# Values of the first pair asked for on two queues, and the loads of keys, queries and weights paced in single pieces

## Chip, cores and metric

One core of a Trainium2 chip runs the whole program. The metric is the device time of one launch in microseconds (us); three runs of the kernel before gave a median of 244.76 us (243.74 to 244.88).

## What is computed

The inputs are 32-bit floats. First comes attention in chunks: each chunk of 32 tokens sees 16 tokens to its left, itself, 8 to its right and 8 memory keys. Then each of the 3072 tokens goes through a dense pair of matrices and through the one expert of eight that a gate picks for it.

```python
for c in range(nc):
    k_ctx = k[:, :, max(0, 32*c - 16):min(S, 32*c + 40)]     # v_ctx alike
    k_full = np.concatenate([mem_k, k_ctx], axis=2)           # v_full alike
    a = softmax(scale * q_c @ k_full.T)
    out[:, :, 32*c:32*c + 32] = a @ v_full
x = out as [3072 tokens, 512]
y = relu(x @ w1_dense) @ w2_dense
e = argmax(x @ w_gate);  p = softmax(x @ w_gate)[e]
y += p * (relu(x @ w1[e]) @ w2[e])
```

Four batches, 8 heads of 64 numbers, 768 tokens in a batch; 8 experts of 512 x 512 and 512 x 512.

## The kernel before

The program has two stages. The **attention stage** is a loop over 24 tiles `i` of 128 tokens (6 to a batch), written as a software pipeline: in round `i` TensorE (PE) makes the scores of tile `i`, turns the exponent's input of tile `i-1` (`turn`), multiplies tile `i-2` with its values (`values`, L612), and turns the finished tile `i-3` for the gate (`turn_x`). Each engine takes its instructions in the order written, and TensorE therefore stops at the first product whose input is late. VectorE (DVE) does the row maxima, subtraction and normalisation (L592, L594, L621, L623), ScalarE (ACT) the exponential (L603) and copies out of PSUM, GpSimd (POOL) the copies in the value tiles and a cast (L629).

**Values.** Two tiles make a pair with one buffer `vw` (four buffers in turn: in the program's lists `vw_133` is the first pair's, `vw_134` the second's, and so on). A pair's values come in eight pieces, four heads in each of two halves (`load_v`, L489; a batch's first pair has four small ones more, L487 and L488), asked for on SyncE's (SP's) queue. Before them `put_mem` (L468) fills the buffer with memory rows on ACT, for the second pair on POOL. The right context of a chunk is the next chunk's rows: `shift_v` copies them inside the buffer, a long copy for either half of the partitions (L505) and, for the pair's last chunk, a short one from the next pair's buffer (L508). The product of the pair's first tile needs its two long copies. That of the second tile needs the two short ones, and so the next pair's values.

**Keys and queries** of a batch (`load_part`, L431) are asked for on POOL, turned to bf16 on the way, and land in `wall`, where later the weights of three experts lie. A batch has 16 pieces of 192 KB, in half-heads: two of keys, two of queries, and the same for the other heads. TensorE turns them a batch ahead (`transposes`, L537), in eight steps per batch, `LATE` for the second batch (two steps in each of rounds 2 to 5), `EVEN` for the others. The first batch's are turned ahead of the loop, with idle products `spin` in between.

**Order.** `pieces` is a list of loads; `piece()` is called four times in a round and issues the next one, or nothing where the entry is `None`. In rounds 0 to 10 `ask_qk` adds two pieces of keys or queries (`QK_AT`), in rounds 12, 13, 15, 17, 19 and 21 `ask_w` adds two pieces of weights (`W_AT`). POOL thus has loads, copies and casts in one line of work.

The **expert stage** takes slots of 128 tokens; each has a dense and an expert half. The products of a slot's second matrices go to two PSUM banks, ACT copies the one to `o`, VectorE adds the other one times the gate's weight (L265), and POOL scatters `o` to the output (L266). The last slot that runs is `tail`.

Of the kernel before, what the change touches and what calls it, by code (L numbers as in the profile page):

```python
# [14 lines left out]
ALU = mybir.AluOpType  # L15
# [40 lines left out]
W_ORDER = [E] + list(range(E))  # L56
W_AT = (12, 13, 15, 17, 19, 21)
QK_AT = tuple(range(11))


@with_exitstack
def kernel(
# [175 lines left out]
    def y_of(j, half):  # L238

        if j == tail and half:  # L240
            return xp[:, 0] if place_of(j) else sc[0]
        return sc[half] if place_of(j) else xp[:, half]
# [16 lines left out]
    def s_exp2(j, w):  # L259
        s_second(j, w, "he", 1)  # L260

    def s_send(j):
        o = w3.tile([128, DM], F32, tag="o", name="o")
        nc.scalar.copy(o, y_of(j, 0))
        nc.vector.scalar_tensor_tensor(o, y_of(j, 1), gws.pop(j), o, op0=ALU.mult, op1=ALU.add)  # L265
        i = nc.gpsimd.indirect_dma_start(  # L266
            out[:, :], bass.IndirectOffsetOnAxis(ap=where.pop(j), axis=0),
            o, None, bounds_check=NTOK - 1, oob_is_err=False)
        for x in sent:
            tc.declare_no_dep(i.ins, x.ins, reason="different rows of out")  # L270
        sent.append(i)
# [131 lines left out]
    with ExitStack() as one:  # L403
# [31 lines left out]

        pieces = []

        def ask_qk():
            if qk_todo:
                a = qk_todo.pop(0)  # L440
                pieces.extend([lambda: load_part(*a, 0, 2), None, lambda: load_part(*a, 2, 2)])

        def ask_w():
            a = w_todo.pop(0)
            pieces.extend([lambda: load_w(*a, 0, 2), None, lambda: load_w(*a, 2, 2)])

# [28 lines left out]

        def load_v(n, half, after=None):
            if n >= B * NP:
# [4 lines left out]
            for hp in range(2 * half, 2 * half + 2):  # L482
                for par in range(2):
                    r = 64 * par
                    if p == 0 and hp == 0:
                        hs_ = v[b].rearrange("(a c) s d -> c s a d", c=2)[par]
                        nc.sync.dma_start(vw[r + LEFT:r + 32, 0, :, :D], hs_[0:LEFT])  # L487
                        nc.sync.dma_start(ves[b][r:r + LEFT, :, :D], hs_[S - LEFT:S])  # L488
                    dma = nc.sync.dma_start(  # L489
                        vw[r:r + 32, lo:, hp, :D],  # L490
# [289 lines left out]
        pool_constants()  # L780
        put_mem(1, nc.gpsimd.tensor_copy)
        load_part(*qk_todo.pop(0), 0, 4)

# [9 lines left out]
        for n, step in enumerate(steps):  # L793
# [6 lines left out]
            if n == 0:  # L800
                put_mem(0, nc.scalar.copy)
            if n == 3:
                load_v(0, 0, i)
                load_v(0, 1)
                load_v(1, 0)
                load_v(1, 1)
                for b in range(1, B):
                    load_mem_rows(b)
# [10 lines left out]
        for i in range(NT):  # L819
# [18 lines left out]
            mine = steps[two[t][0]:two[t][1]] if steps else []  # L838
            if i in QK_AT:
                ask_qk()  # L840
            if i in W_AT:
                ask_w()
            piece()
            if i % 2 == 0:
                if i:
                    load_v(i // 2 + 1, 1, tiles[i - 3]["pace"] if i > 3 else None)
            else:
                load_v(i // 2 + 2, 0)
# [13 lines left out]
            do("turn", 1)  # L862
            if mine:
                mine[0]()
            if ga:
                gate(ga)
            do("turn_x", 3)
            if mine[1:]:
                mine[1]()
# [25 lines left out]
            if gd and gd["n"] < EG - 1:  # L895
                add_up(gd)
            for step in mine[2:]:
                step()
            if 1 <= i <= E:
                last_constants(i - 1)  # L900
            piece()
            if i < NT - 2:
                shift_v(i // 2, i % 2, False, nc.scalar.copy if i == 1 else nc.gpsimd.tensor_copy)
            if i % 2 == 0:
                put_mem(i // 2 + 2, nc.scalar.copy)
            if i == 1:
                for e in range(E):
                    nc.gpsimd.tensor_copy(wgp[:, :, e:e + 1], wgr[:, :, PERM[e]:PERM[e] + 1])
            if NT - 3 <= i < NT - 1:
# [117 lines left out]
```

## Time and profile before

| what | value |
|---|---|
| runs, median (range) | 244.76 us (243.74 to 244.88) |
| the profiled execution's own time | 243.71 us |
| its span, first to last instruction | 242.0 us |
| PE, DVE, ACT, POOL busy | 87%, 60%, 57%, 68% |
| mean granted TensorE clock | 0.959 |
| DMA | 35.46 MB in packets, 147 GB/s |
| values in the chain that ended last (DMA `vw`) | 9% of the span |

A busy share is a mean over both stages; each stretch has its own limit. The attention stage fills about the first 130 us, the expert stage the rest. Where a row names an engine after an arrow, that is what the waiting instruction waited for last. Queue q0 carries what POOL asks for, q1 what SP asks for.

### The profile page before, as it was taken

To read this page: it belongs to the slowest core of one execution; us is meant where nothing else is said; L and a number is where in the kernel's file an instruction comes from. 1 tells how busy PE (TensorE), PEld (TensorE's weight loads), DVE (VectorE), ACT (ScalarE), POOL (GpSimd) and SP (SyncE) were. 2 spreads that over 40 slices of the span, in tenths; PEclk is the share of its full clock that TensorE was granted. 3 is DMA by queue.
4 is the path that set the end of the run, shared out by engine and by line. 5 is a ranking of instruction groups with operands and counts; after the bars stand their busy time and mean duration, and the time that the engine had idled before them with its cause. 6 is when DMAs were issued, how large, how long until landed. Compare 5 with 4: busy or idle time off the path is not lost.

```text
span 242.0 us, 9891 instructions
## 1 busy us (share of the span) xinstructions
PE 210.0 (87%) x4093; PEld 152.5 (63%) x4093; DVE 144.8 (60%) x413; ACT 137.0 (57%) x201; POOL 165.7 (68%) x228
## 2 busy tenths in 40 slices
PE   8874899887977978867889988989999999999990
PEld 3443676665755756655667766667777777777750
DVE  7656577476555856938967577366533425666650
ACT  6863977977849759516543355433444544444440
POOL 7943999969938956979596048787777653764332
PEclk9999799999979799979799999999999999999997
DMA  5997999997994983896539715999999980322112
GB/s 71 181 166 149 154 195 169 190 164 114 200 163 87 219 134 75 132 234 111 123 91 187 167 60 122 171 205 209 258 186 218 230 226 17 144 81 77 55 43 82
DMA packets 52515, 35.46 MB, mean 147 GB/s; under 512 B 29676, under 2 KB 50158, under 8 KB 52464
## 3 DMA queue, kind: packets, MB, share of 16 engines
q0 software_dynamic: 22080, 25.22, 57.8%
q1 hardware_dynamic: 30384, 9.54, 17.6%
q8 instruction: 34, 0.56, 1.0%
q14 instruction: 17, 0.14, 0.2%
HBM read 41.45 MB, written 10.24 MB: 214 GB/s over the span
## 4 chain that ended last, share of the span: by engine, by line
PE 46%; DMA 16%; DVE 11%; POOL 9%; issue 8%; SPq 4%; ACT 3%; POOLq 0%; DVEq 0%; ACTq 0%
DMA vw<-in_v_dram 9%; PE xp L247 8%; PE xtp L232 7%; PE ap L232 7%; PE sc L247 6%; PE xp L612 5%; POOL vw L505 4%; DMA out_dram<-o,idx 3%; SPq L489 3%; PE xtp L633 2%; PE ap L601 2%; DMA wall<-in_q_dram 2%; DMA xg<-xs,ixt 2%; PE tp L218 2%; DVE xn L623 2%
## 5 line engine op out<-in xcount | busy, mean ns | idle before, releaser
L232 PEld LDWEIGHTS <-wall 128*128 128x128 bf16 x672 | 40.4, 98 | 6.4 <-issue 0.4
L505 POOL COPY vw<-vw 24x1820 f32<-24x1820 f32 x21 | 35.6, 1696 | 8.6 <-DMA vw<-in_v_dram 7.5
L612 PE MATMUL xp<-vw,aT 64*32 64x65 f32 x1536 | 27.5, 234 | 12.5 <-POOL vw L508 5.2
L612 PEld LDWEIGHTS xp<-vw,aT 64*32 64x32 f32 x1536 | 20.1, 110 | 19.7 <-POOL vw L508 7.2
L235 ACT ACTIVATE hd<-ap 128x512 bf16<-128x512 f32 x26 | 15.5, 597 | 28.8 <-PE ap L232 27.6
L220 DVE COPY xT<-tp 128x512 bf16<-128x512 bf16 x24 | 10.2, 423 | 32.7 <-PE tp L218 31.5
L232 PE MATMUL ap<-xT,wall 128*128 128x128 bf16 x416 | 27.5, 219 | 0.0
L235 ACT ACTIVATE he<-xtp 128x512 bf16<-128x512 f32 x26 | 15.6, 598 | 14.8 <-PE xtp L232 14.7
L266 POOL DMA_INDIRECT out_dram<-o,ixt x12 | 13.6, 1137 | 15.0 <-DVE o L265 10.9
L603 ACT ACTIVATE aT<-ap 128x512 f32<-128x512 f32 x24 | 14.4, 599 | 15.3 <-PE ap L601 15.3
L621 DVE RECIPROCAL rs<-xp 128x8 f32<-128x8 f32 x24 | 5.0, 206 | 28.6 <-PE xp L612 28.6
L468 ACT COPY vw<-memt 128x2080 f32<-128x2080 f32 x11 | 21.3, 1935 | 0.1
L537 PEld LDWEIGHTS <-wall 128*64 128x64 bf16 x384 | 12.6, 116 | 10.4 <-issue 5.7
L202 POOL DMA_INDIRECT xg<-xs,ixt x12 | 12.8, 1066 | 8.9 <-PE ap L232 5.8
L546 ACT COPY kt<-tp 64x768 bf16<-64x768 bf16 x22 | 17.4, 791 | 2.0 <-PE tp L537 1.7
L601 PE MATMUL ap<-identf,a 128*128 128x128 f32 x96 | 17.7, 313 | 0.9 <-DVE low L178 0.5
L633 PE MATMUL xtp<-identf,xn 128*128 128x128 f32 x96 | 17.3, 309 | 0.9 <-DVE xn L623 0.5
L623 DVE TENSOR_TENSOR xn<-xp,rs 128x512 f32<-128x512 f32 x24 | 16.6, 692 | 2.3
L113 POOL DMA_DIRECT2D wall<-in_moe_w_dram x23 | 17.7, 778 | 0.0
L629 POOL CAST rows<-xn 128x512 bf16<-128x512 f32 x24 | 14.7, 619 | 3.8 <-DVE xn L623 1.9
L594 DVE TENSOR_TENSOR a<-sc,mx 128x512 f32<-128x512 f32 x24 | 16.6, 691 | 0.8
L592 DVE TENSOR_REDUCE mx<-sc 128x8 f32<-128x512 f32 x24 | 16.4, 683 | 0.3
(163 smaller groups left out, 470.8 us busy)
## 6 DMA issues: line engine op xcount, KB each, us to landing
wall<-in_moe_w_dram POOLq DMA_DIRECT2D x9, 512.0 KB, 8.8
vw<-in_v_dram SPq DMA_DIRECT2D x64, 64.0 KB, 4.3
wall<-in_moe_w_dram POOLq DMA_DIRECT2D x14, 256.0 KB, 6.3
xs<-rows SPq DMA_DIRECT2D x6, 514.0 KB, 4.8
wall<-in_q_dram POOLq DMA_DIRECT2D x16, 192.0 KB, 5.9
wall<-in_k_dram POOLq DMA_DIRECT2D x14, 192.0 KB, 4.9
vw<-in_v_dram SPq DMA_DIRECT2D x32, 56.0 KB, 5.1
wall<-in_moe_w_dense_dram POOLq DMA_DIRECT2D x4, 256.0 KB
```

The costliest lines, as they stand in the source:

```text
L113: nc.gpsimd.dma_start(wall[:, e, DT * half + t0:DT * half + t0 + nt], src.rearrange("(t p) m -> p t m", p=128)[:, t0:t0 + nt])
L232: nc.tensor.matmul(ph[:, f, :], w[:, d, 128 * f:128 * f + 128], xT[:, d, :], start=(d == 0), stop=(d == DT - 1))
L235: nc.scalar.activation(h, ph, AF.Relu)
L247: nc.tensor.matmul(y_of(j, half), h[:, f, :], w[:, f, :], start=(f == 0), stop=(f == FT - 1))
L468: copy(vws[n].rearrange("p c h d -> p c (h d)"), memt[:, n // NP].rearrange("p h d -> p (h d)").unsqueeze(1) .to_broadcast([128, PC, HP * ...
L505: eng(vw[r + 32:r + 56, :PC - 1], vw[r:r + 24, 1:])
L546: done.append(eng(kt[r, hp, par, LEFT:LEFT + S].rearrange("d (p i) -> d p i", i=TPB), turned[r]))
L594: nc.vector.tensor_tensor(a.rearrange("p h q m -> p (h q) m"), scv, mx.unsqueeze(2).to_broadcast([128, H, KEYS]), ALU.subtract)
L601: nc.tensor.transpose(ap[:, hp, :], st["a"][:, hp], identf)
L612: nc.tensor.matmul(xp[32 * cc:32 * cc + 32, par, (D + 1) * hp:(D + 1) * (hp + 1)], st["aT"][r, hp, 32 * cc:32 * cc + 32], vw[r, 4 * (g % 2 ...
L623: st["pace"] = nc.vector.tensor_tensor(xn.rearrange("p (h a d) -> p a h d", a=2, d=D), xv[:, :, :, :D], rs.unsqueeze(3).to_broadcast([128, ...
L633: nc.tensor.transpose(xtp[:, d, :], st["xn"][:, 128 * d:128 * d + 128], identf)
```

## The change

The second half of the first pair's values is asked for on POOL's queue, ahead of its fill of the second pair's buffer and of the second batch's keys and queries; the first half stays on SP. POOL's fill and those loads come behind it in the code. ACT copies the first pair's second half of the partitions in round 0 instead of 1, ahead of the first exponential, and fills the third pair's buffer in round 1 instead of 0; that pair's first half is asked for after this fill. In round 2 the two turning steps come behind the values product. Eight small POOL copies (`wgp`) become five on VectorE. Keys, queries and weights are asked for by numbers: `QK_PIECES` gives the pieces of keys and queries added in rounds 0 to 14 (2, 0, 3, 3, 1, 1, 2, ...), and from round 10 on a round with fewer than two adds one piece of weights until there are twelve. The second product of the last slot goes to two banks by halves of 256 columns, and VectorE adds each by itself.

```diff
--- before.py
+++ after.py
@@ -54,8 +54,8 @@
 NVB = 4
 NXG = 6
 W_ORDER = [E] + list(range(E))
-W_AT = (12, 13, 15, 17, 19, 21)
-QK_AT = tuple(range(11))
+QK_PIECES = (2, 0, 3, 3, 1, 1, 2, 1, 1, 2, 1, 1, 2, 1, 1)
+W_FROM, W_PIECES = 10, 12
 
 
 @with_exitstack
@@ -236,9 +236,6 @@
         hs[j, nm] = h
 
     def y_of(j, half):
-
-        if j == tail and half:
-            return xp[:, 0] if place_of(j) else sc[0]
         return sc[half] if place_of(j) else xp[:, half]
 
     def s_second(j, w, nm, half):
@@ -257,12 +254,24 @@
         s_second(j, wall[:, E, DT:], "hd", 0)
 
     def s_exp2(j, w):
-        s_second(j, w, "he", 1)
+        if j != tail:
+            return s_second(j, w, "he", 1)
+        h = hs.pop((j, "he"))
+        for x, y in enumerate(y_parts(j)):
+            for f in range(FT):
+                nc.tensor.matmul(y, h[:, f, :], w[:, f, 256 * x:256 * x + 256],
+                                 start=(f == 0), stop=(f == FT - 1))
+
+    def y_parts(j):
+        return (xp[:, 0] if place_of(j) else sc[0])[:, :256], ap.rearrange("p a n -> p (a n)")[:, :256]
 
     def s_send(j):
         o = w3.tile([128, DM], F32, tag="o", name="o")
         nc.scalar.copy(o, y_of(j, 0))
-        nc.vector.scalar_tensor_tensor(o, y_of(j, 1), gws.pop(j), o, op0=ALU.mult, op1=ALU.add)
+        gw = gws.pop(j)
+        for x, y in enumerate(y_parts(j) if j == tail else [y_of(j, 1)]):
+            part = o[:, 256 * x:256 * x + 256] if j == tail else o
+            nc.vector.scalar_tensor_tensor(part, y, gw, part, op0=ALU.mult, op1=ALU.add)
         i = nc.gpsimd.indirect_dma_start(
             out[:, :], bass.IndirectOffsetOnAxis(ap=where.pop(j), axis=0),
             o, None, bounds_check=NTOK - 1, oob_is_err=False)
@@ -433,16 +442,29 @@
                 src[b, 4 * h + n0:4 * h + n0 + n].rearrange("h (p i) d -> p h (i d)", p=128))
 
 
-        pieces = []
-
-        def ask_qk():
-            if qk_todo:
-                a = qk_todo.pop(0)
-                pieces.extend([lambda: load_part(*a, 0, 2), None, lambda: load_part(*a, 2, 2)])
-
-        def ask_w():
-            a = w_todo.pop(0)
-            pieces.extend([lambda: load_w(*a, 0, 2), None, lambda: load_w(*a, 2, 2)])
+        pieces, qk_parts, w_parts = [], [], []
+
+        def plan(i):
+            n = QK_PIECES[i] if i < len(QK_PIECES) else 0
+            mine = []
+            for _ in range(n):
+                if not qk_parts and qk_todo:
+                    a = qk_todo.pop(0)
+                    qk_parts.extend(lambda a=a, x=x: load_part(*a, x, 2) for x in (0, 2))
+                if qk_parts:
+                    mine.append(qk_parts.pop(0))
+            if i >= W_FROM and n < 2 and w_count[0] < W_PIECES:
+                if not w_parts:
+                    a = w_todo.pop(0)
+                    w_parts.extend(lambda a=a, x=x: load_w(*a, x, 2) for x in (0, 2))
+                mine.append(w_parts.pop(0))
+                w_count[0] += 1
+            for p in mine:
+                pieces.extend([p, None])
+            if pieces and pieces[-1] is None:
+                pieces.pop()
+
+        w_count = [0]
 
         def piece():
             if pieces:
@@ -473,7 +495,7 @@
             tc.add_manual_dep(dma.ins, ins.ins.name, mybir.DependencyInfo(
                 mybir.DependencyClass.Sync, mybir.DependencyReason.DATA), reason="pace")
 
-        def load_v(n, half, after=None):
+        def load_v(n, half, after=None, queue=nc.sync):
             if n >= B * NP:
                 return
             b, p = divmod(n, NP)
@@ -486,7 +508,7 @@
                         hs_ = v[b].rearrange("(a c) s d -> c s a d", c=2)[par]
                         nc.sync.dma_start(vw[r + LEFT:r + 32, 0, :, :D], hs_[0:LEFT])
                         nc.sync.dma_start(ves[b][r:r + LEFT, :, :D], hs_[S - LEFT:S])
-                    dma = nc.sync.dma_start(
+                    dma = queue.dma_start(
                         vw[r:r + 32, lo:, hp, :D],
                         bass.AP(tensor=v.tensor,
                                 offset=v[b, 2 * hp + par, CHUNK * (PC * p + lo) - LEFT, 0].offset,
@@ -778,8 +800,6 @@
         nc.vector.memset(wgp, 0.0)
         make_identity(nc, identf)
         pool_constants()
-        put_mem(1, nc.gpsimd.tensor_copy)
-        load_part(*qk_todo.pop(0), 0, 4)
 
 
         def spin(n):
@@ -799,9 +819,11 @@
             i = step(four[n % 4], two[n > 1:] if n % 2 else two)
             if n == 0:
                 put_mem(0, nc.scalar.copy)
+                load_v(0, 1, queue=nc.gpsimd)
+                put_mem(1, nc.gpsimd.tensor_copy)
+                load_part(*qk_todo.pop(0), 0, 4)
             if n == 3:
                 load_v(0, 0, i)
-                load_v(0, 1)
                 load_v(1, 0)
                 load_v(1, 1)
                 for b in range(1, B):
@@ -836,15 +858,12 @@
             tiles[i]["grp"], tiles[i]["u"] = grps[i // G], i % G
             two = LATE if b == 0 else EVEN
             mine = steps[two[t][0]:two[t][1]] if steps else []
-            if i in QK_AT:
-                ask_qk()
-            if i in W_AT:
-                ask_w()
+            plan(i)
             piece()
             if i % 2 == 0:
                 if i:
                     load_v(i // 2 + 1, 1, tiles[i - 3]["pace"] if i > 3 else None)
-            else:
+            elif i > 1:
                 load_v(i // 2 + 2, 0)
             if i >= 3 and (i - 3) % G == 0:
                 grps[(i - 3) // G]["rows"] = work.tile([128, G, ROW], F32, tag="rows", name="rows", bufs=3)
@@ -860,12 +879,12 @@
             if gc and gc["n"] == EG - 1:
                 mark(gc, range(2, G))
             do("turn", 1)
-            if mine:
+            if mine and i > 2:
                 mine[0]()
             if ga:
                 gate(ga)
             do("turn_x", 3)
-            if mine[1:]:
+            if mine[1:] and i > 2:
                 mine[1]()
             if i == 0:
                 constants()
@@ -894,18 +913,24 @@
                 mark(gc, range(G))
             if gd and gd["n"] < EG - 1:
                 add_up(gd)
-            for step in mine[2:]:
+            for step in mine[2 if i > 2 else 0:]:
                 step()
             if 1 <= i <= E:
                 last_constants(i - 1)
             piece()
-            if i < NT - 2:
-                shift_v(i // 2, i % 2, False, nc.scalar.copy if i == 1 else nc.gpsimd.tensor_copy)
-            if i % 2 == 0:
+            if i < NT - 2 and i != 1:
+                shift_v(i // 2, i % 2, False, nc.gpsimd.tensor_copy)
+            if i == 0:
+                shift_v(0, 1, False, nc.scalar.copy)
+            if i == 1 or i % 2 == 0 and i:
                 put_mem(i // 2 + 2, nc.scalar.copy)
             if i == 1:
-                for e in range(E):
-                    nc.gpsimd.tensor_copy(wgp[:, :, e:e + 1], wgr[:, :, PERM[e]:PERM[e] + 1])
+                load_v(2, 0)
+            if i == 1:
+                for e in range(4):
+                    nc.vector.tensor_copy(wgp[:, :, e:e + 1], wgr[:, :, PERM[e]:PERM[e] + 1])
+                assert PERM[4:] == list(range(4, E))
+                nc.vector.tensor_copy(wgp[:, :, 4:E], wgr[:, :, 4:])
             if NT - 3 <= i < NT - 1:
                 shift_v(B * NP - 1, i % 2 == 0, False, nc.scalar.copy)
             for par in range(2):
```


POOL's line of work behind the last of its constants, ahead of and in the first rounds of the loop (`wall` takes keys and queries, `memt` holds the memory rows), before:

```order
L468 COPY vw_134<-memt 128x2080
L431 DMA wall<-in_k_dram 128x4x384
L431 DMA wall<-in_q_dram 128x2x384 x2
L505 COPY vw_133<-vw_133 24x1820
L431 DMA wall<-in_k_dram 128x2x384 x2
L908 COPY wgp<-wgr 128x4 x8
L431 DMA wall<-in_q_dram 128x2x384 x2
L505 COPY vw_134<-vw_134 24x1820
L508 COPY vw_133<-vw_134 24x260 x2
```

and with the change:

```order
L511 DMA vw_133<-in_v_dram 32x7x64 x4
L490 COPY vw_134<-memt 128x2080
L440 DMA wall<-in_k_dram 128x4x384
L440 DMA wall<-in_q_dram 128x2x384 x2
L527 COPY vw_133<-vw_133 24x1820
L440 DMA wall<-in_k_dram 128x2x384 x2
L527 COPY vw_134<-vw_134 24x1820
L530 COPY vw_133<-vw_134 24x260 x2
L440 DMA wall<-in_q_dram 128x2x384
```

The four asks for values are new at the head; the copies of `wgp` are gone, two asks for queries that stood ahead of the second pair's long copy stand behind the short ones, and one more of keys is not there yet.

ACT's line of work from the last copy ahead of the loop (`aT` is the exponential), before:

```order
L542 COPY qT_201<-ap 128x768
L468 COPY vw_135<-memt 128x2080
L603 ACTIVATE aT<-ap 128x512
L505 COPY vw_133<-vw_133 24x1820
L603 ACTIVATE aT<-ap 128x512
L546 COPY kt_126<-tp 64x768
L542 COPY qT_352<-sc_72 128x768
```

and with the change:

```order
L564 COPY qT_199<-ap 128x768
L527 COPY vw_133<-vw_133 24x1820
L625 ACTIVATE aT<-ap 128x512
L490 COPY vw_135<-memt 128x2080
L625 ACTIVATE aT<-ap 128x512
L568 COPY kt_126<-tp 64x768
L564 COPY qT_352<-sc_72 128x768
```

The first pair's copy moves ahead of the first exponential, and the fill of `vw_135` from ahead of it to behind it.

## Rows read from the trace of the kernel before

**Rows 1.** The page: its first line

```profile
span 242.0 us, 9891 instructions
```

**Rows 2.** Waits of 0 to 50 us: who waited for what, us in total, times, longest

```profile
DVE rs L621 <- PE xp L612: 10.6, 6, 3.0
POOL vw L505 <- DMA vw<-in_v_dram: 7.5, 1, 7.5
```

**Rows 3.** Timeline of POOL: start us, us, instruction, count, idle before and releaser

```profile
10.67 1.91 POOL L468 COPY vw<-memt 128x2080 f32<-128x2080 f32 x1
12.53 0.79 POOL L431 DMA_DIRECT2D wall<-in_k_dram  x1
13.32 1.41 POOL L431 DMA_DIRECT2D wall<-in_q_dram  x2
22.25 1.69 POOL L505 COPY vw<-vw 24x1820 f32<-24x1820 f32 x1 [7.52 <-DMA vw<-in_v_dram]
...
25.35 1.06 POOL L908 COPY wgp<-wgr 128x4 f32<-128x4 f32 x8
...
27.80 1.69 POOL L505 COPY vw<-vw 24x1820 f32<-24x1820 f32 x1
29.45 0.85 POOL L508 COPY vw<-vw 24x260 f32<-24x260 f32 x2
...
31.00 0.61 POOL L629 CAST rows<-xn 128x512 bf16<-128x512 f32 x1
```

**Rows 4.** DMA queues, 14.9 to 18.5 us: packets, MB, share of 16 engines

```profile
q0 software_dynamic: 864, 0.64, 120.9%
q1 hardware_dynamic: 56, 0.01, 3.0%
```

**Rows 5.** DMA queues, 28 to 31.2 us

```profile
q0 software_dynamic: 575, 0.41, 88.7%
q1 hardware_dynamic: 846, 0.20, 35.1%
```

**Rows 6.** SP's queue: eight asks for values

```profile
26.51 3.78 SPq L489 DMA_DIRECT2D vw<-in_v_dram  x8
```

**Rows 7.** Line 489's asks, 0 to 60 us: ask to landing

```profile
DMA to landing us min/median/max: 1.9/3.6/5.5
```

**Rows 8.** Timeline of ACT

```profile
18.39 0.60 ACT L603 ACTIVATE aT<-ap 128x512 f32<-128x512 f32 x1 [1.26 <-PE ap L601]
22.36 1.70 ACT L505 COPY vw<-vw 24x1820 f32<-24x1820 f32 x1 [3.37 <-DMA vw<-in_v_dram]
```

**Rows 9.** Timeline of PE: values products of tiles 0, 1 and 9

```profile
24.00 1.30 PE L612 MATMUL xp<-vw,aT 64*32 64x65 f32 x64 [2.54 <-POOL vw L505]
...
30.35 0.80 PE L612 MATMUL xp<-vw,aT 64*32 64x65 f32 x50 [0.16 <-POOL vw L508]
...
65.35 0.80 PE L612 MATMUL xp<-vw,aT 64*32 64x65 f32 x50 [0.15 <-POOL vw L508]
```

**Rows 10.** Windows: us; busy PE, PEld, DVE, ACT, POOL; granted clock, DMA share, GB/s

```profile
22.25:65.97 43.72, 36.68 (x1138) 27.56 (x1138) 26.44 (x88) 36.70 (x48) 40.61 (x58) 0.96 1.03 168
...
31.20:66.20 35.00, 30.78 (x959) 23.04 (x958) 23.22 (x78) 28.30 (x39) 32.03 (x42) 1.00 1.05 172
```

**Rows 11.** Waits of 31.2 to 66.2 us, all engines

```profile
POOL oh_sum L694 <- issue: 1.9, 1, 1.9
PE xp L612 <- POOL vw L508: 1.9, 6, 0.9
...
PE xp L612 <- POOL vw L505: 0.6, 1, 0.6
```

**Rows 12.** The page, part 6: DMA issues, KB each, us to landing

```profile
wall<-in_q_dram POOLq DMA_DIRECT2D x16, 192.0 KB, 5.9
```

**Rows 13.** Timeline of the end, all engines

```profile
234.83 0.59 ACT L264 COPY o<-xp 128x512 f32<-128x512 f32 x1 [0.59 <-PE xp L247]
...
235.75 0.75 DVE L265 SCALAR_TENSOR_TENSOR o<-sc,gw,o 128x512 f32<-128x512 f32 x1 [0.73 <-PE sc L247]
```

## The prediction

> **What bounds the kernel now.** I read the waits of the first 50 us first: they are the program's fill, and nothing stands ahead of it. The longest is POOL's, 7.5 us for the first pair's values [rows 2]. POOL's timeline gives its place: asks for the second batch's keys and queries end at 14.73, and the first long copy starts at 22.25 [rows 3]. The queues tell why so late. From 14.9 to 18.5 us the keys and queries on q0 moved 0.64 MB and the values on q1 0.01 MB [rows 4]; the values had been asked for before, and stood. Then I read TensorE: the first values product starts at 24.00 after 2.54 us of waiting for that copy, the second ends at 30.35 + 0.80 = 31.15, the tenth (tile 9) at 66.15 [rows 9].
>
> Between those two, POOL is the bound with TensorE close behind: POOL is busy 40.6 of 43.7 us, TensorE 30.8 of 35.0 [rows 10], and TensorE's wait for POOL's copies comes to 1.9 + 0.6 = 2.5 us [rows 11]. A delay of POOL at the start therefore runs on through ten tiles. What counts is when POOL starts the long copy in the second pair's buffer (call it S, 27.80 now [rows 3]), since the second tile's product needs the two short copies behind it (S + 1.65 + 0.85), and everything on POOL follows in line.
>
> **The head, step by step.** POOL is free for the four new asks at 10.67 [rows 3]. An ask of 192 KB takes it 1.41 / 2 = 0.71 us; four take 2.8. The fill of the second pair's buffer (1.9) then ends at 15.4, the asks for keys and queries (0.79 + 1.41) at 17.6. No row shows a value ask on POOL. By bounds, it is not below the shortest ask there, and the longest, 0.79, would add 0.3; I take 0.71, whose number of rows is like this one's. The first pair's second half is now ahead of the second batch's keys in one queue, and the first half has q1 with no keys beside it until about 17.8 (before, they fill the window that begins at 14.9, 2.4 us after their ask at 12.53; now they are asked for at 15.4). So the pair should be in by 16 to 17, and POOL's copy starts at 17.6, held by POOL's own line. ACT's copy (1.70 [rows 8]) runs ahead of the first exponential (0.60), from about 16.5 to 18.2, and the exponential, which starts at 18.39 now, is hardly pushed back. The first product starts at 17.6 + 1.7 = 19.3 or shortly after, not at 24.00. If the first half stood on q1 as long as before, ACT and the exponential would stand with it.
>
> **The second pair is late next.** SP may ask for it once POOL's fill is done, at 15.4; eight asks take 3.78 [rows 6], so until 19.2. The shortest landing seen is 1.9 [rows 7], which gives S = 21.1 as the early end. The late end: nothing of it moves while keys do. They are 0.77 MB, and 0.38 more that POOL asks for right behind its first copy, at 19.3 to 20.7; at q0's 0.64 / 3.6 = 0.18 MB/us that is 6.5 us from 17.8, so 24.3, and 0.51 MB of values behind them at a like rate is 2.8 more: S = 27. Between these lies the sharing of 28 to 31.2 us, when q1 moved 0.20 MB in 3.2 us beside 0.41 on q0 [rows 5]: the two or three pieces asked for first come ahead of the keys, and 0.32 MB at 0.062 MB/us take 5.1 us from 17.8. That gives 23, and one more for a start as in [rows 4]: **S = 24**, nearest to the row with both queues at work. It is 3.8 us earlier than 27.80.
>
> [...]
>
> **From the second tile to the tenth.** Counted in the order of instructions, between S and the short copies of round 10 there are now 14 asks on POOL, and were 16; at 0.71 that is 1.4 us less. Copies and casts (0.61) stay as many. TensorE can gain at most its 2.5 us of waiting. I count 0.4 for both: with POOL ahead, TensorE's own line is the limit for some tiles, and POOL then waits in round 8 for the rank that TensorE makes (`oh_sum`), as it does now for 1.9 us [rows 11]. So the tenth product ends about 4.2 us earlier, near 62.
>
> **The rest of the edits.** The `wgp` copies leave POOL (1.06 us [rows 3]); there they would now lie in the wait for the second pair, so this is worth nothing. On VectorE five of them cost at most about 1 us, beside its waiting for the products, 3.0 at the longest [rows 2]; without that cover they would delay a normalisation by as much. The fill of the third pair's buffer comes after the first exponential, and that pair is first copied in round 4, at S + 2.5 + 4.4 + 2.0, some 9 us after S. The turning steps of round 2 come behind the product, which waits no longer for them. After round 10, POOL has 14 asks in rounds 11 to 22 and had 12; it waits for TensorE there and has room. I carry the 4.2 us to the end, since the stage behind is the same work in the same order.
>
> **The last slot.** ACT's copy ends at 235.42, VectorE's 0.75 starts at 235.75 [rows 13] when all products are done. By halves, the first can start at 235.45. A half costs between 0.375 and 0.75; I take 0.45, near the half, since the columns are halved. The second half then ends at 236.35 or, if it must wait for its products, at 235.75 + 0.45 = 236.2, and not at 236.50: I take 0.2 us (0.3 at the best; 0.45 lost if a half cost as much as the whole). [...]
>
> **Sum.** 3.8 + 0.4 + 0.2 = 4.4 us. Against the profiled execution's 243.71 this is 239.3. The median of the runs is 1.05 above that execution (its span of 242.0 [rows 1] plus 1.7 around it), so the median should be 244.76 - 4.4 = **240.4 us**; the forecast's own range, S from 23 to 25.2, is 239.2 to 241.8.
>
> **Rivals.**
> - *The second pair comes early (S about 21).* Its pieces get through in the gap before the keys move. 6.8 + 0.4 + 0.2 = 7.4, so 237.4; with half of TensorE's waiting gone too, 236.5. For it: landings of 1.9 us occur. Against: [rows 4].
> - *It stands behind the keys (S 26 to 27).* 1.8 + 0.2 = 2.0, so 242.8, at the worst 243.8. For it: [rows 4]. Against: [rows 5].
> - *Only issue time is saved.* The bytes to be moved before the first product are the same; if the engines serve both queues alike, the pair arrives with the keys whichever queue asked. SP is spared four asks, 3.78 / 2 = 1.9 us, and with the end's 0.2 that is 242.7. [...] Against it: within q0 the order is the order of asking, and [rows 4] show the queue's order deciding.
> - *Slower: the later queries arrive late.* The pieces of the last two batches are asked for two to three rounds ahead of their turn with the change, and three or more before it. The tightest is the first query piece of the third batch: on POOL at S + 2.5 + 4.4 (round 3: three asks, cast, copy) + 1.3 (round 4: cast, ask) = 32.2. It is turned halfway through TensorE's round 6, which begins with the end of tile 3's product at 36.0 (the second product ends at S + 2.5 + 0.8 = 27.3, and eight more take 35.0 now [rows 10], so two some 8.7); half a round more is 38.2. That leaves 6.0 us. Queries take 5.9 us to land [rows 12]. TensorE's line would stop at each turn that is late. With landings 3 us longer it loses 2.8 there and about 0.5 at each of the other seven query pieces of the last two batches, 6 in all, and the time is 246.4. It decides from a landing of about 8.5 us on. Against it: there are fewer asks per round, so landings should shorten.
> - *No change.* The gain is given back after round 10, where POOL waits for TensorE's rank and TensorE for POOL's copies: 244.6.
>
> **How the numbers follow.** Forecast 0.47; early pair 0.18; late pair 0.15; issue time only 0.07; late queries 0.07; given back 0.06. A measurement of this kernel tells about 0.5% from no change, 1.2 us. Below 243.5 lie the forecast, the early pair, 0.11 of the late one and 0.05 of issue time only: 0.81 faster. Slower is the 0.07 of late queries, the same is the rest, 0.12. The range leaves out late queries, the given-back case and the outer ends of both pair cases, together some 0.18: 236.5 to 243.7.
>
> **What would show it.** POOL's first long copy near 17.6 and the first product near 19.3; the second pair's long copy near 24, with POOL waiting for values some 3 us ahead of it; the tenth product's end near 62; hardly any waits of turning steps for loads. Wrong would be: the first copy still after 20 (the queue's order does not decide); S outside 21 to 27; the tenth product early and the expert stage's start not; TensorE waiting for `wall` in rounds 6 to 17.

## The result and the profile after

In one series on one chip the changed kernel took **242.3 us** in the median (238.69 to 248.56, 22 runs), the kernel before 244.82 (241.75 to 249.51, 22 runs). Medians here are over all runs, disturbed runs are left out of every ratio that has an interval, and of the profiles the first pair's and those of the halves alone, the 38 products more and the constants early without halves are undisturbed. The ratio is **0.9881 (95% interval 0.9852 to 0.991)**: 1.2% faster, 2.9 us where 4.4 were forecast (the two medians differ by 2.5). The profiled execution took 241.26 us against 243.71, so 2.45 of it can be looked up. Most of its lines stand 22 higher in this part of the code: L612 is now L634, L505 L527, L508 L530, L489 L511; L431 is L440.

The page, first line:

```profile
span 239.4 us, 9877 instructions
```

POOL's timeline, which answers to [rows 3] (start us, us, instruction, count, idle before and releaser):

```profile
10.97 2.46 POOL L511 DMA_DIRECT2D vw<-in_v_dram  x4 [0.27 <-issue]
13.43 1.93 POOL L490 COPY vw<-memt 128x2080 f32<-128x2080 f32 x1
15.30 0.79 POOL L440 DMA_DIRECT2D wall<-in_k_dram  x1
...
17.58 1.69 POOL L527 COPY vw<-vw 24x1820 f32<-24x1820 f32 x1
...
24.64 1.69 POOL L527 COPY vw<-vw 24x1820 f32<-24x1820 f32 x1 [4.00 <-DMA vw<-in_v_dram]
26.28 0.85 POOL L530 COPY vw<-vw 24x260 f32<-24x260 f32 x2
```

POOL does what was forecast: the first long copy at 17.58 and not at 22.25, the second pair's (S) at 24.64 and not at 27.80, with a wait of 4.0 us for values ahead of it. Yet the first product gained only 1.55 us. The timeline of all engines, 17 to 23 us, has the reason:

```profile
17.09 1.70 ACT L527 COPY vw<-vw 24x1820 f32<-24x1820 f32 x1 [1.20 <-DMA vw<-in_v_dram]
...
18.09 1.30 DVE L166 CAST cols<-iot 128x192 bf16<-128x192 int32 x1
...
21.06 0.69 DVE L616 TENSOR_TENSOR a<-sc,mx 128x512 f32<-128x512 f32 x1
...
21.90 0.63 PE L623 MATMUL ap<-identf,a 128*128 128x128 f32 x4 [1.80 <-DVE low L178]
...
22.45 0.86 PE L634 MATMUL xp<-vw,aT 64*32 64x65 f32 x64
```

Both copies are done at 19.27, but on TensorE tile 1's `turn` (L623) stands ahead of tile 0's product, and it waits for VectorE, which is held up by the program's constants (`constants()`, L166 to L174): the first cast takes 1.30 us.

TensorE's products of tiles 1, 9 and 23, which answer to [rows 9] (of each the last row; an end is start plus duration):

```profile
27.88 0.75 PE L634 MATMUL xp<-vw,aT 64*32 64x65 f32 x48 [0.40 <-issue]
...
65.81 0.80 PE L634 MATMUL xp<-vw,aT 64*32 64x65 f32 x50 [0.16 <-POOL vw L530]
...
124.70 0.85 PE L634 MATMUL xp<-vw,aT 64*32 64x65 f32 x64
```

Tile 23's product of the kernel before, from the same view:

```profile
127.67 0.85 PE L612 MATMUL xp<-vw,aT 64*32 64x65 f32 x64
```

So tile 1 ends at 28.63 (31.15 before, 2.5 us earlier), tile 9 at 66.61 (66.15: **0.5 later**), tile 23 at 125.55 (128.52: 3.0 earlier). In this pair of profiles the head's gain was gone at the tenth tile, and what the result has came in the 14 rounds after it. What differs in this pair are TensorE's waits, from 14 to 66.2 us before and to 66.4 after (engine, line, waited for: us in total, times, longest). Before:

```profile
PE xp L612 <- POOL vw L505: 3.1, 2, 2.5
PE xp L612 <- POOL vw L508: 3.0, 8, 0.9
PE xp L612 <- issue: 1.3, 2, 1.0
```

and after:

```profile
PE xp L634 <- issue: 5.4, 5, 2.1
PE ap L623 <- DVE low L178: 1.8, 1, 1.8
PE xp L634 <- POOL vw L527: 0.6, 1, 0.6
PE xp L634 <- POOL vw L530: 0.6, 3, 0.2
```

The waits for POOL fell from 6.1 to 1.2 us, and stops for which the profile names no releaser grew from 1.3 to 5.4, inside the products. The longest of them, timeline of TensorE in the changed kernel:

```profile
36.12 0.63 PE L634 MATMUL xp<-vw,aT 64*32 64x65 f32 x37
38.80 0.45 PE L634 MATMUL xp<-vw,aT 64*32 64x65 f32 x27 [2.06 <-issue]
```

The DMA queues from 36.3 to 38.9 us hold, beside loads, one packet on the queue that carries instructions; it begins at 36.5, 2.3 us ahead of the stop's end:

```profile
q0 software_dynamic: 366, 0.26, 66.1%
q1 hardware_dynamic: 1168, 0.28, 58.4%
q8 instruction: 1, 0.02, 2.1%
```

The same holds for the other stops in tiles 1 to 6: those that end at 27.88, 32.96, 48.46 and 53.49 end 2.2 to 2.6 us after such a packet begins. In the kernel before a packet lies at 35.1, and the product that runs 2.3 us later stood then for POOL anyway:

```profile
37.43 0.33 PE L612 MATMUL xp<-vw,aT 64*32 64x65 f32 x12
38.11 0.30 PE L612 MATMUL xp<-vw,aT 64*32 64x65 f32 x2 [0.35 <-POOL vw L508]
38.57 0.80 PE L612 MATMUL xp<-vw,aT 64*32 64x65 f32 x50 [0.16 <-POOL vw L508]
```

My reading of this one pair, **theory 1**: TensorE's own instructions come too late; while it waited for POOL, their load was hidden, and once POOL was early it showed. **Theory 2**: POOL's line, or the head, still sets the pace, the head's gain is carried, and the loss at the tenth tile has another cause.

From the tenth tile on, busy time and granted clock (window, us, busy PE, PEld, DVE, ACT, POOL, clock, DMA share, GB/s), before and after:

```profile
66.20:128.50 62.30, 51.19 (x1509) 38.95 (x1509) 43.22 (x130) 37.22 (x54) 46.83 (x62) 0.89 0.72 136
```

```profile
66.60:125.60 59.00, 49.36 (x1510) 37.95 (x1510) 44.01 (x130) 37.05 (x54) 48.92 (x65) 0.91 0.84 154
```

Of the 3.3 us, 1.8 are busy time of the same products: the granted clock stood at 0.50 for 13.7 us of the stretch before (from 68.4, 78.6, 105.9 and 116.1) and for 10.3 after (from 74.0 and 108.1). The same stretch takes 63.7 and 67.9 us in the change's other two profiles, of other series, so how much of the 3.3 us the change itself brought this pair cannot tell. The other 1.5 are waits. Before:

```profile
PE xp L612 <- POOL vw L508: 2.2, 4, 1.4
PE misc L743 <- DVE on L737: 2.0, 1, 2.0
...
PE xp L612 <- POOL vw L505: 0.9, 1, 0.9
```

After:

```profile
PE sc L604 <- issue: 4.5, 3, 2.1
...
PE xp L634 <- POOL vw L530: 0.4, 2, 0.3
...
PE xp L634 <- POOL vw L527: 0.2, 1, 0.2
```

The end, before and then after (beside [rows 13]): the last slot's second product, its sums, its scatter:

```profile
234.63 1.03 PE L247 MATMUL sc<-wb,he 128*128 128x512 bf16 x4
...
236.77 0.97 POOL L266 DMA_INDIRECT out_dram<-o,ixt  x1 [0.51 <-DVE o L265]
```

```profile
231.49 0.60 PE L262 MATMUL sc<-wb,he 128*128 128x256 bf16 x4
...
231.93 0.60 PE L262 MATMUL ap<-wb,he 128*128 128x256 bf16 x4
...
232.31 0.48 DVE L274 SCALAR_TENSOR_TENSOR o<-sc,gw,o 128x256 f32<-128x256 f32 x1 [0.43 <-ACT o L270]
232.71 0.47 DVE L274 SCALAR_TENSOR_TENSOR o<-ap,gw,o 128x256 f32<-128x256 f32 x1
233.95 0.97 POOL L275 DMA_INDIRECT out_dram<-o,ixt  x1 [0.83 <-DVE o L274]
```

From the product's start, the sum ends after 1.69 us (1.87 before), as forecast; but the scatter begins after **2.46** (2.14 before). The gap between sum and scatter grew from 0.27 to 0.77 us; why, no row tells.

### The profile page after: what moved, and what is told of

The parts are those of the page before. It is cut to its first block, busy times and chain, and to the rows that moved or that the text cites. A ratio compares the mean times of both kernels' runs of the same rounds, so it can differ in the third digit from the quotient of the medians.

```text
span 239.4 us, 9877 instructions
## 1 busy us (share of the span) xinstructions
PE 205.7 (86%) x4078; PEld 151.1 (63%) x4097; DVE 146.9 (61%) x419; ACT 137.1 (57%) x201; POOL 167.7 (70%) x224
## 3 DMA queue, kind: packets, MB, share of 16 engines
q1 hardware_dynamic: 29424, 9.31, 17.6%
## 4 chain that ended last, share of the span: by engine, by line
PE 50%; DVE 16%; DMA 13%; issue 10%; POOL 7%; SPq 1%; ACT 1%; POOLq 0%; DVEq 0%; ACTq 0%
PE xp L244 8%; PE xtp L232 8%; PE ap L232 7%; PE sc L244 6%; PE xp L634 5%; DMA out_dram<-o,idx 3%; PE xtp L655 3%; DMA vw<-in_v_dram 3%; DMA wall<-in_k_dram 2%; PE ap L623 2%; DVE xn L645 2%; DMA xg<-xs,ixt 2%; PE tp L218 2%; PE tp L559 2%; PE misc L667 2%
## 5 line engine op out<-in xcount | busy, mean ns | idle before, releaser
L527 POOL COPY vw<-vw 24x1820 f32<-24x1820 f32 x21 | 35.6, 1696 | 5.1 <-DMA vw<-in_v_dram 4.0
L634 PE MATMUL xp<-vw,aT 64*32 64x65 f32 x1536 | 25.4, 232 | 7.7 <-issue 5.8
L220 DVE COPY xT<-tp 128x512 bf16<-128x512 bf16 x24 | 10.2, 423 | 32.4 <-PE tp L218 31.2
L634 PEld LDWEIGHTS xp<-vw,aT 64*32 64x32 f32 x1536 | 19.0, 109 | 14.1 <-issue 10.1
L275 POOL DMA_INDIRECT out_dram<-o,ixt x12 | 13.3, 1108 | 14.7 <-DVE o L274 10.3
L559 PEld LDWEIGHTS <-wall 128*64 128x64 bf16 x384 | 12.7, 116 | 11.8 <-issue 5.1
L623 PE MATMUL ap<-identf,a 128*128 128x128 f32 x96 | 16.9, 303 | 2.4 <-DVE low L178 1.8
L655 PE MATMUL xtp<-identf,xn 128*128 128x128 f32 x96 | 17.3, 308 | 1.0 <-DVE xn L645 0.5
```

The source lines that it names most:

```text
L527: eng(vw[r + 32:r + 56, :PC - 1], vw[r:r + 24, 1:])
L559: nc.tensor.transpose(tb[64 * par:64 * par + 64, i, :], src[:, par, D * i:D * i + D], ident, tile_position=(0, 64 * par))
L623: nc.tensor.transpose(ap[:, hp, :], st["a"][:, hp], identf)
L634: nc.tensor.matmul(xp[32 * cc:32 * cc + 32, par, (D + 1) * hp:(D + 1) * (hp + 1)], st["aT"][r, hp, 32 * cc:32 * cc + 32], vw[r, 4 * (g % 2 ...
L655: nc.tensor.transpose(xtp[:, d, :], st["xn"][:, 128 * d:128 * d + 128], identf)
```

## Experiments

They ran in three series, each on one chip, where the kernel before took 254.66, 254.75 and 254.26 us; only ratios to it in the same series are compared. Where "medians" stands, the runs gave no interval, and the ratio is that of the two medians.

| series | kernel | median us (runs) | ratio (95%) |
|---|---|---|---|
| 1 | head alone | 253.79 (12) | 0.9943 (0.9879 to 1.0007) |
| 1 | pacing alone | 252.15 (12) | 0.9882 (0.9828 to 0.9936) |
| 1 | halves alone | 255.06 (12) | 1.008 (1.0015 to 1.0145) |
| 1 | whole asks | 261.96 (6) | medians: 1.029 |
| 2 | change | 252.56 (12) | medians: 0.991 |
| 2 | fill first | 252.61 (12) | 0.9879 (0.9802 to 0.9956) |
| 2 | constants early | 251.03 (12) | 0.9826 (0.9725 to 0.9927) |
| 2 | 38 products more | 253.75 (12) | 1.0045 (0.9968 to 1.0122) |
| 3 | pacing alone | 251.47 (13) | 0.9974 (0.9929 to 1.002) |
| 3 | change without halves | 251.79 (6) | 0.9829 (0.9744 to 0.9914) |
| 3 | the same, constants early | 251.31 (6) | medians: 0.988 |
| 3 | change | 250.41 (7) | 0.9846 (0.9767 to 0.9925) |

### One part of the change at a time

The change has three parts that can be taken singly. Pacing alone is the kernel before with

```diff
-W_AT = (12, 13, 15, 17, 19, 21)
-QK_AT = tuple(range(11))
+QK_PIECES = (2, 0, 3, 3, 1, 1, 2, 1, 1, 2, 1, 1, 2, 1, 1)
+W_FROM, W_PIECES = 10, 12
...
-            if i in QK_AT:
-                ask_qk()
-            if i in W_AT:
-                ask_w()
+            plan(i)
```

halves alone is the kernel before with the new `s_exp2`, `y_parts` and `s_send`, and head alone is the change with both of these undone.

> Only the head of the change: first pair on two queues, POOL's order and ACT's order at the loop's start, the turning steps of round 2 behind the product, wgp on VectorE. Pacing and last slot as before. Theory 1 (TensorE's own stops, with no releaser in the profile, take the place of its waits for POOL within ten rounds; the net gain of the change comes from the pacing): 244.0 to 244.8 us against 244.8 before, ratio 0.997 to 1.0, second product's end near 28.6, tenth's near 66. Theory 2 (the head's 2.5 us at the second product are carried to the end, the tenth product's late end in the one profile is chance): 242.2 to 242.8, ratio 0.990 to 0.992.

> Only the pacing of keys, queries and weights by the numbers; head and last slot as before. Theory 1: 242.2 to 243.0 us, ratio 0.990 to 0.993, with TensorE's waits for POOL's copies between 66 and 130 us down from 3.1 us to under 1. Theory 2: 244.3 to 244.8, ratio 0.998 to 1.0.

> Only the last slot's product in halves. Both theories: 0.2 us less, ratio 0.999 (0.998 to 1.001); in the profile the last addition on VectorE ends 0.2 to 0.3 us after ACT's and TensorE's last end less late than before. A half of the addition 0.40 to 0.50 us.

The head alone, at 0.9943, lies between what the theories gave. The pacing alone, at 0.9882, went further than theory 1 had it, and its waits for POOL's copies from 66 to 130 us are down to 0.4 us, as theory 1 expected.

With the head alone TensorE stops without a releaser in the same products as with the whole change: after 16 of tile 1, 26 of tile 2, 37 of tile 3, 41 of tile 5, 63 of tile 6, and after 49 of tile 4 besides; from 24 to 66 us these stops come to 5.5 us. Only those in tiles 1 and 2, 1.8 us here and 1.1 with the change, are seen with the early head alone; the others it did not bring. The halves alone, whose head and pacing are those of before, stop after 37 products of tile 3, 48 of tile 4 and 62 of tile 6; their waits from 14 to 66.4 us, their stop in tile 3 and their tenth product:

```profile
PE xp L621 <- issue: 4.0, 3, 1.7
...
40.36 0.45 PE L621 MATMUL xp<-vw,aT 64*32 64x65 f32 x27 [0.92 <-issue]
...
68.53 1.28 PE L621 MATMUL xp<-vw,aT 64*32 64x65 f32 x64
```

The pacing alone stops for 3.0 us there, two times. So the 1.3 us of the kernel before are the least of all profiles with the old head, and the tenth product, at 66.15 there, ends at **69.81** with the same head and pacing (at 67.93 with the head alone, in the same series). From the second product's end to the tenth's, this work takes 35.0 us in the kernel before, 39.0 in the halves alone and 38.0 in the change. The loss at the tenth tile can therefore be the kernel before's good profile as well as the stops: that the stops took what the head saved, the second half of theory 1, is not shown.

With the pacing alone, S is at 25.46 (25.92 in its second profile, below). The halves alone, whose head and pacing are those of before, have it at 27.19 and the kernel before at 27.80, so **the pacing alone makes S 1.3 to 2.3 us earlier**: two asks for queries (1.4 us) no longer stand ahead of it. With the head alone it is at 24.65, the same as with both (3.2 us). Head and pacing relieve the same line, and what POOL no longer spends on asks it waits for values (2.59 us ahead of S with the head alone, 4.00 with both). The second product ends, in single profiles, at 31.15 and 30.81 with neither, 29.71 with the head, 28.81 and 29.26 with the pacing, 28.64 to 29.19 with both: the pacing alone gives most of that gain. It has a price: with the pacing alone a turning step in round 4 waits 2.40 us for queries that are now asked for later; in the change that wait is 0.56.

The halves alone lose where a gain of 0.1% was expected. Their profile has the change's end: the scatter begins 2.47 us after the second product does, against 2.14 or 2.15 in every kernel without halves. That is 0.3 us, or 0.13%, just below the interval's lower end of 0.15%; the rest of the 0.8% no row explains, and the two medians, 255.06 and 254.66, differ by 0.16%.

### Fewer asks on POOL

```diff
-                    qk_parts.extend(lambda a=a, x=x: load_part(*a, x, 2) for x in (0, 2))
+                    qk_parts.extend([lambda a=a: load_part(*a, 0, 4), None])
...
-                    w_parts.extend(lambda a=a, x=x: load_w(*a, x, 2) for x in (0, 2))
+                    w_parts.extend([lambda a=a: load_w(*a, 0, 4), None])
```

> The changed kernel, but each pair of neighbouring pieces of keys, queries or weights is one ask of twice the size at the first one's place: 11 asks fewer of keys and queries and 6 fewer of weights on POOL, some 0.6 us each, 10 us of POOL's line in the attention stage. Theory 1 (TensorE's own stops are the bound now, POOL is not): 241.5 to 242.5 us against 242.3 for the change, POOL idle instead. Rival (POOL's line is still the bound in the rounds): 238 to 240.

17 asks fewer, and both theories missed: 2.9% slower. POOL had more room (157.3 us busy against 167.7) and the kernel lost, so its time for asks does not set the pace here, against theory 2. But theory 1's "unchanged" fell too, and an ask of twice the size changes more than POOL's line: a turning step waits 2.5 us for queries. TensorE's waits from 24 to 135 us:

```profile
PE xp L634 <- issue: 7.3, 8, 2.5
PE sc L604 <- issue: 6.8, 3, 3.2
PE misc L667 <- issue: 2.8, 1, 2.8
```

The longest of these again end 2.4 to 2.5 us after an instruction packet begins. What makes them longer no row tells.

### The same instructions, 38 products earlier in the stream

```diff
-        spin(9)
+        spin(5)
+        for _ in range(42):
+            nc.tensor.matmul(bank(xp[:, 0])[:, 0, :32], ones, ones[:, :32], start=True, stop=True)
```

Idle products ahead of the loop; their results are not used. 42 are added and 4 taken away.

> The changed kernel with 42 products of 32 columns (84 TensorE instructions) in place of four idle ones of 512 columns ahead of the first turning step; nothing else moves. If TensorE's stops without a releaser are loads of its own instructions, they stay 2.3 to 2.6 us behind a packet of the instruction queue q8 and come 84 instructions earlier in the program: the one after 37 products of the fourth values group (2.06 us in the changed kernel) falls at the last products of the turning step ahead of that group, the one after 26 of the third group in the step ahead of that one. If they are made by the loads of data at that time, they stay at their places in the program. Time within 0.5% of the changed kernel's either way.

Timeline of TensorE (the two turning steps L559 of 12 products, the transposes L655 of 4 and the product follow each other in a round):

```profile
28.01 0.36 PE L559 MATMUL tp<-ident,wall 128*64 128x128 bf16 x6 [2.23 <-issue]
...
36.87 0.52 PE L559 MATMUL sc<-ident,wall 128*64 128x128 bf16 x11
37.73 0.22 PE L559 MATMUL sc<-ident,wall 128*64 128x128 bf16 x1 [0.34 <-issue]
```

The stop after 16 of tile 1's products now falls ahead of the last 6 of the first turning step: 6 + 4 + 12 + 16 = 38. That after 37 of tile 3's falls one product ahead of them: 1 + 37 = 38. Those after 41 in tile 5 and 63 in tile 6 fall after 3 and 25. **These four stops moved by exactly the 38 products put in**, in front of other operations with other inputs; the one after 26 of tile 2 has no counterpart. (The expectation's 84 instructions leave out the four products taken away and their loads.) The stops belong to places in TensorE's own stream and not to POOL, values or loads: this half of theory 1 is shown. The time was 0.5% above the change's by the medians, the most that was expected.

### POOL's fill ahead of the four asks, and the constants ahead of the first tile

```diff
+                put_mem(1, nc.gpsimd.tensor_copy)
                 load_v(0, 1, queue=nc.gpsimd)
-                put_mem(1, nc.gpsimd.tensor_copy)
```

> The changed kernel with POOL's fill of the second pair's buffer ahead of the four asks for the first pair's second half, so that SP can ask for the second pair 2.5 us earlier. Expected of both theories: the second pair's first long copy starts 1 to 2.5 us earlier than in the changed kernel (24.6). Theory 1 (TensorE's own stops take the place of its waits for POOL): the tenth product ends within 0.7 us of the changed kernel's, total ratio to before within 0.003 of the changed kernel's. Theory 2 (the head's gain is carried): 1 to 2.5 us less than the changed kernel.

S came 0.65 us earlier than the changed kernel's 24.64, at 23.99 (0.9 against the same series), less than the 1 to 2.5 expected; the tenth product ended at 66.0 and the median is that of the change. The other one calls `constants()` ahead of the loop:

```diff
+        constants()
...
-            if i == 0:
-                constants()
```

> The changed kernel with the casts of constants on VectorE ahead of the loop instead of in round 0, so that they run before POOL's first long copy. If the 1.30 us of the first cast in the changed kernel (0.25 before) come from POOL copying in SBUF at the same time, the casts take 0.25 each here wherever POOL is not copying, and the first values product starts 1 to 2 us earlier than in the changed kernel (22.45), near 20.5 to 21.4; if they come from something else, the first cast stays above 1 us. The second product waits for the second pair either way: total within 0.3% of the changed kernel's.

The first product starts at 20.61, as expected, 1.8 us earlier than with the change, and the tenth ends at 65.72. What that says depends on the profile of the change that it is held against: 66.61 in the first, 67.8 in this series, 65.5 in the next. One kernel's tenth product moves by 2 us from profile to profile, and neither edit's gain can be followed so far. The median is 0.6% below the change's where 0.3% at most was expected; the runs do not tell the two apart. The cast only met another copy of POOL: it ran from 14.11 for 1.41 us, and POOL's fill from 13.47 for 1.93.

> The changed kernel once more, on the chip of these runs, as the one to compare with. Ratio to the kernel before 0.985 to 0.992 by both theories.

### Together, without the halves

The change with the old `s_exp2` and `s_send`, and then `constants()` early too; beside them, once more, pacing alone and the change.

> The pacing of keys, queries and weights alone, a second time, as the measure for the next kernel on the same chip. Both theories: a ratio of 0.988 to the kernel before (0.984 to 0.992), last scatter 2.15 us after the second half product begins.

> The change without the halves in the last slot: new head and new pacing. Theory 1 (what the head saves is given back to TensorE's own instruction loads by the tenth tile, so only the pacing counts): within 0.003 of the pacing alone, 0.986 to 0.990. Theory 2 (the head's saving is carried to the end, about 0.994 by the run of the head alone, and is eaten by the halves): the product of the two, 0.982, that is 1.5 us faster than the pacing alone. By both the last scatter begins 2.15 us after the second half product begins, where the change has 2.46.

> The last kernel, with the constants' casts on VectorE put ahead of the first turning step, so that no cast stands beside GpSimd's long copy. Both theories: first product near 20.6 us, where the change has 22.45. Theory 1: the tenth tile's product ends at 65.5 to 66.5 us all the same, total 0.982 to 0.988. Theory 2: it ends near 64.5 and the total is 0.975 to 0.980.

> The change unaltered, as the measure on the same chip: 0.988 (0.984 to 0.992). If the halves cost what the trace shows (last scatter 2.46 us after the second half product begins, against 2.14), it lies 0.3 us, 0.1%, above the kernel without them, which is too little to be told apart; if they cost what the run of the halves alone showed (0.8%), it lies 2 us above it.

Pacing alone came out at 0.9974, outside what both theories expected, and the change without halves at 0.9829. That contradicts theory 1's claim that only the pacing counts, and is what theory 2 gave (0.982). It is weak evidence: the second ratio rests on three of the six runs, the two intervals all but touch (0.9914 and 0.9929), and the medians over all runs, 251.47 and 251.79, show no gain at all. With the constants early the first product started at 20.57 and the tenth ended at 62.50 + 0.80 = 63.3, earlier than theory 2 had it and 2.2 to 4.5 us ahead of the change's three. But with the halves, which differ only in the last slot, the same early constants gave 65.72, so single profiles of the same work differ as much; the total was within 0.5 us of the kernel without that edit, in theory 1's range and not in theory 2's. With and without halves differ by less than the intervals. No version was shown to beat the change.

The run without halves also shows more of the slow cast. VectorE and, below, POOL:

```profile
17.30 0.30 DVE L166 CAST cols<-iot 128x192 bf16<-128x192 int32 x1
...
17.65 1.67 DVE L168 CAST slot<-iot 128x29 f32<-128x29 int32 x1
```

```profile
17.57 1.71 POOL L518 COPY vw<-vw 24x1820 f32<-24x1820 f32 x1
```

Here the 192-column cast came ahead of POOL's copy and took 0.30 us; a cast of 29 columns behind it took 1.67 and ended at 19.32, 0.04 after the copy. The long time is not the 192-column cast's own: here the 29 columns took it, which in the change, begun at 19.45 with the copy over, took 0.17.

## Why the prediction was right or wrong

- **Where POOL's first copy goes: right.** 17.6 was forecast and 17.58 measured; four value asks took 2.46 us, 0.62 each where I took 0.71.
- **S: right.** 24 was forecast and 24.64 measured. From 17.1 to 24.6 us q1 moved 0.47 MB, 0.063 MB/us, beside 0.96 MB on q0; the row I chose, [rows 5], had given 0.062. Here both queues were at work, with 1966 packets on q1 against 1307 on q0, where [rows 4] have 56 against 864. The 23 that this rate gave without the late start is 1.6 us early.
- **"The first product starts at 17.6 + 1.7 = 19.3 or shortly after": wrong by 3.2 us.** I followed the copies and ACT and left out VectorE. The turn of tile 1 stands between, and behind VectorE's constants; before, they had been over long ahead of the product, hidden by the wait for POOL.
- **"The tenth product ends about 4.2 us earlier, near 62": the step that failed.** It ended 0.5 us later in the pair of profiles, and at 65.5 to 67.8 in the change's three; none is near 62. I put down to POOL what TensorE waited for (2.5 us of 35 [rows 11]) and took what was left, from one profile, as TensorE's own line at work. That line has stops of its own, 5.4 us in 14 to 66 us with the change and 1.3 in the profile that I read, but 4.0 in the halves alone with the same head and pacing. The 35.0 us between second and tenth product, which I took as given, were 38.0 with the change and 39.0 in the halves alone. Whether the early head lengthens this stretch, or the profile before was a good one, stays open. All three low-clock stretches of the changed kernel from 39 us to the last values product begin within 1.1 us of such a stop (39.9 after 38.80, 74.0 after 73.39, 108.1 inside the 2.10 us that end at 108.72).
- **"I carry the 4.2 us to the end": wrong in its working.** There was nothing to carry in this pair, and 3.3 us were gained after the tenth tile, where I had counted zero for the new pacing: fewer waits for POOL's copies (3.1 to 0.6 us) and a higher clock, which no run lays to the change. The total fell into the range by luck: 2.9 against 4.4 is nearer than its steps, whose errors went both ways.
- **Head and pacing as separate terms:** S = 24 came from the head in my sum; the head alone gives all of it (24.65), but the pacing alone gives most of it too (25.46), so the two do not add.
- **The last slot: wrong sign.** A half took 0.47 us, where 0.45 was estimated, but the scatter follows the sum half a microsecond later than before, so 0.2 gained became 0.3 lost.
- **The rivals.** Queries: landing 5.6 us, and TensorE waited for them only once in the loop, 0.6 us in round 4, for the second batch's; not what happened. "Given back" put the loss behind round 10; in this pair the gain was gone before the tenth tile's end, and to what is open.

Shown are the late first product and its cause, the gain at the second product and that the pacing alone gives most of it, the places of the stops, and the later scatter of the halves. Not shown is what the stops cost the change, nor how the 1.2% divides between head and pacing: the pacing alone measured 0.988 and 0.997, the head alone 0.994, and whether a gain of the head reaches the end came out differently in the second and third series.

## What to carry to other kernels

A wait that is taken away is not all gain. Look first whether the *waiting* engine has stops of its own, as TensorE had here (5.4 us in 14 to 66.4 us), and in which places of the stream. Before taking a stretch's length from one profile, take several of the same kernel: here the same work took 35.0 and 39.0 us, as much as the whole forecast gain apart. Ahead of the first use of an input, follow every engine whose instruction stands in front of the consumer in its order, small constants included. Splitting the last operation is worth only what its last consumer lets through: measure from the product's start to the store, not to the sum.

## What the hardware showed

**TensorE's stops and the packets on the instruction queue.** The page has 34 packets, 0.56 MB, on q8, a queue of instructions, some 16 KB each. From 66.6 to 125.6 us there are 12, beside 1510 products with 1510 weight loads (the window above): 126 products to a packet. Counted in the order of products, the six places of the head alone (16 of tile 1 to 63 of tile 6) lie 126 to 128 products apart. In every profile most stops without a releaser end 2.2 to 3.0 us after such a packet begins. That the packets hold TensorE's instructions is my inference from these counts; no row names an engine for them. The 64 tiny products of a tile take 0.86 us with their loads, and the packets begin 3.3 to 6.1 us apart in 25 to 66 us; why a packet begins early enough at one place and late at the next no row tells.

**The first cast on VectorE ended with POOL's copy.** In the nine profiles where it met POOL's copy or fill, the first cast took 0.40 to 1.75 us instead of 0.25 and ended 0.1 us after that copy or fill. In the change without halves the cast of 29 columns did, with 1.67 us beside the copy and 0.17 for the same cast alone. The reductions and subtractions that read PSUM took no longer beside the same copies: with the constants early 0.68 and 0.69 us at 18.24 and 18.95, and as much at 20.15 and 20.87 with no copy on POOL. Why the casts ended with the copy no row tells.

**From series to series the same kernel differs by 4%.** The kernel before took 244.8 us on one and 254 to 255 in the three series of experiments. Much of it lies behind the last values product: 113.8 us from its end to the end of the span in the first profile of the change, 119.9 in the halves alone, 121.1 with the 38 products.
